# Attention and two MLPs on one core: a planner with shorter bookings for ScalarE and VectorE, and phase three's tanh by halves through one PSUM bank

## The chip, the core and the metric

The kernel runs on one core of a Trainium2 chip. TensorE (PE in the profile) multiplies, VectorE (DVE), ScalarE (ACT) and GpSimd (POOL) work on tiles, and SyncE (SP) issues the transfers; each takes its own instructions strictly in program order. PSUM, where TensorE's products land, is used here as eight banks of 512 fp32 columns. The metric is the device time in microseconds, the median of several executions.

## What is computed

```python
kv = np.einsum('bhsd,bhse->bhde', k, v)            # 8 batches, 8 heads, 576 x 64
out = np.einsum('bhsd,bhde->bhse', q, kv)
rms = np.sqrt(np.mean(out * out, axis=-1, keepdims=True) + 1e-06)
x = (out / rms * g_norm)                           # as 4608 tokens x 512
h = x @ w_in;  x = np.maximum(0.01 * h, h) @ w_out # first MLP, 512 -> 2048 -> 512
h = x @ w_in2; x = (h - np.tanh(h)) @ w_out2       # second MLP
```

## The kernel before

The work stands in four phases, one per weight matrix. Phase one multiplies the normalized attention output by w_in and applies the leaky maximum; phase two multiplies by w_out; phase three multiplies by the second w_in and subtracts the tanh; phase four multiplies by the second w_out. Tokens go in strips of 288 (phases one and two, two strips per batch) or 256 (three and four). Each block product is done with seven products instead of eight, as Strassen does, and each fp32 operand is split into two fp16 parts, a high and a low one, so that a product is three fp16 matmuls per pair of blocks.

The names in the rows: `opa` and `ops` are the split left operands of a strip (ScalarE writes the high part, L576 or L578, VectorE the low one, L583 or L585). `ps_a` to `ps_d` are the PSUM banks that products go to. What a later sum still needs of `ps_a` is copied out by ScalarE (`keep`, L694 to L698: tiles `c`, `u` and `g`); VectorE adds the other banks to those copies (`add`, L707, into `g`). In phase one a bank for `ps_a` comes round again after three products, in phase three too. `wo` is a split of a weight block (ScalarE's high part at L518, `unit` being its input, of which POOL forms differences at L498 to L502).

The attention of batch b is put between phase one's products: `kvd` (L967) is ScalarE's copy of k's product with v, `qt` (L986) its copies of the turned q, `po` (L997) TensorE's product of both, `sq` its square. When a batch is through, the reciprocal roots (`iv`) are written to memory, loaded again spread over the heads (`bc`, L1073), and POOL multiplies the batch's `xg` by them, block by block (L1079, `scale`); then `opa` and `ops` are made from `xg` for that batch's strips.

The order of every engine's program is set at build time by a planner, the class `Plan`. `fit` books a stretch of an engine's calendar for each operation: `dur` is the time that it's given, `over` by how much it may overlap its neighbour, and the operation goes into the first gap that is long enough. `chain` books a list of steps one after the other; each list entry is (engine, duration, function, overlap), "A", "V" and "G" for ScalarE, VectorE and POOL, and None for a pure delay such as a transfer (`LOADBC`, 8 us for `bc`). A function that finds no room in a pool raises NoRoom and is tried again a little later. Instructions are issued in the order of the booked times, so the numbers decide orders and nothing else.

Phase three's strip function is `tanh` (L1423): one ScalarE instruction takes the tanh of four blocks (128x1024) into a tile `th` of the pool L in SBUF, and VectorE subtracts it from `g` in two instructions of 128x512 (L1432). In phase three the banks 0 to 6 hold products; bank 7 is idle there, and phase four uses it.

Of the kernel before, what the change touches and what calls it, by code (L numbers as in the profile page):

```python
# [11 lines left out]
F32 = mybir.dt.float32  # L12
I32 = mybir.dt.int32
AF = mybir.ActivationFunctionType
ALU = mybir.AluOpType
# [14 lines left out]
NOP = 7  # L30
P = 128
# [17 lines left out]
class Plan:  # L49
# [2 lines left out]

    HAND, OVER = 0.25, {"A": 0.6, "V": 0.35, "G": 0.35}

    def __init__(self, delays, dry):
# [9 lines left out]
    def fit(self, eng, t, dur, over=0.0):  # L67


        taken = self.taken[eng]  # L70
        k = max(0, bisect.bisect(taken, (t, 0.0)) - 1)
        while k < len(taken) and taken[k][0] < t + dur - over:
            t = max(t, taken[k][1])
            k += 1
        while k < len(taken) and taken[k][0] < t:
            k += 1
        taken.insert(k, (t, t + dur))
        return t
# [147 lines left out]
def lay_out(plan, nc, pools, sizes, args):  # L226
    q, k, v, g_norm, w1, w2, w3, w4, out = args
    B, H, S, D, NT, DM, DFF = sizes
    NP = DFF // P // 2
# [4 lines left out]
    T2 = 256  # L234
# [8 lines left out]
    L, M, X = (Slots(plan, work, kind, n) for kind, n in (("l", NL), ("m", NM), ("x", NX)))  # L243
    at = plan.at

    used = set()

    def bank(n, name):
        if n in used:
            plan.miss(("bank", n))  # L250
        used.add(n)
        return ps.tile([P, 512], F32, tag=f"p{n}", name=name)

    def free(n):
        used.discard(n)
        plan.met(("bank", n))
# [570 lines left out]
    LOADBC, LOADBC1 = 8.0, 9.0  # L827
# [119 lines left out]
    def pair(b, c, held):  # L947
# [92 lines left out]
        def m_after(e):  # L1040
            if c == PAIRS[-1]:
                norms(b, e)
# [8 lines left out]
    def norms(b, e):  # L1051
        held = {}
# [16 lines left out]
        def load(kk):  # L1069
            held[kk] = L.take([P, 4, T1], F32, "bc", True)  # L1070
            rows = ivd[b].rearrange("(w q) t -> q w t", q=Q)
            for h in range(2):
                nc.sync.dma_start(  # L1073
                    out=held[kk].ap[D * h:D * h + D], in_=rows[2 * kk + h:2 * kk + h + 1].broadcast_to((D, 4, T1))
                )

        def scale(kk, e, n0, n1):
            x = xg[b, kk].ap[:, n0:n1]
            e.tensor_tensor(out=x, in0=x, in1=held[kk].ap[:, n0:n1], op=ALU.mult)  # L1079
            if n1 == 4:  # L1080
                L.give(held[kk])

        x0ops[b] = [{}, {}]
        more = []
        for kk in range(2):
            stages = left_stages(
                lambda kk=kk: xg[b, kk].ap, x0ops[b][kk], None, T1, over=lambda kk=kk: L.give(xg[b, kk]), pieces=2,
                first=None if b else "V", rest=None if b else "V", over_s=() if b else (SOVER,),
            )
            if b == 1:  # L1090
                scaled_ = [("V", 0.66, lambda kk=kk, n=n: scale(kk, nc.vector, n, n + 2)) for n in (0, 2)]
            else:
                scaled_ = [("G", 0.76, lambda kk=kk, n=n: scale(kk, nc.gpsimd, n, n + 1)) for n in range(4 if b else 1)]
            more.append([(None, LOADBC if b > 1 else LOADBC1 if b else 6.0, lambda kk=kk: load(kk))] + scaled_ + stages)

        def wide(kk, n):
            k_ = (4 * kk + n) % 4
# [61 lines left out]
    t = 1.0  # L1159
# [7 lines left out]
    for o in order:  # L1167
        if o[0] == "a":
            held = {}
# [52 lines left out]
    for hp in range(4):  # L1222
        c = PAIRS[hp]
        t_, held = ta[0, c]
# [12 lines left out]
    FIRST = {1: (None,) * EARLY + (0, 8, 16, 24)[:4 - EARLY], 2: (14, 25, 36, 47), 3: (60, 72, 84, 96)}  # L1237
# [3 lines left out]
    for b in range(1, B):  # L1241
        for hp in range(4):
            c = PAIRS[hp]
            n0 = FIRST[b][hp] if b in FIRST else NOP * (NP * b - 16 + 2 * hp) - 2 * (b - 4)
            if n0 is None:
                continue
            held = ta[b, c][1] if (b, c) in ta else {}
            for (dur, fn, after), o in zip(pair(b, c, held), OFFS.get(b, (1, 4, 6, 8, 10, 13))):
                extra.setdefault(n0 + o, []).append((dur, fn, after))
            if b > 1:  # L1250
                loads.append((n0 - 13, b, c, held))
# [168 lines left out]
    spread(lambda i, kk, t: split_late(2, i, kk, t, L, M), UNITS, end1 + 45.0, end2 - 28.0)  # L1420


    def tanh(g, s):  # L1423
        held = {}

        def one():
            held["t"] = L.take([P, 4, T2], F32, "th", True)
            nc.scalar.activation(out=held["t"].ap, in_=g(), func=AF.Tanh)  # L1428

        def two(n):  # L1430
            o = g()[:, 2 * n:2 * n + 2]
            nc.vector.tensor_tensor(out=o, in0=o, in1=held["t"].ap[:, 2 * n:2 * n + 2], op=ALU.subtract)  # L1432

        return [
            ("A", 1.15, one),
            ("V", 0.7, lambda: two(0)), ("V", 0.7, lambda: two(1)),
            (None, 0.0, lambda: L.give(held["t"])),
        ]

    def banks2(n):  # L1440
# [7 lines left out]

    state["rest"] = second_scales(whole, NS2, end2 + 12.0)
    up(1, T2, NS2, x1ops, tanh, lambda s: consts[s][1:3], banks2, ORDER2, between2, freed_to(3, 0.4))  # L1450
    end3 = plan.pe
    c3 = end2 + 0.45 * (end3 - end2)
# [77 lines left out]
```

## Time and profile before

| | |
|---|---|
| time, median of 3 runs | 1490.52 us (1490.04 to 1491.99) |
| profiled execution, its own time | 1495.29 us |
| its span, first to last instruction | 1493.5 us |
| TensorE busy | 1443.8 us (97%), mean granted clock 0.986 |
| VectorE, ScalarE, GpSimd busy | 1245.4 us (83%), 933.7 us (63%), 599.8 us (40%) |

TensorE is busy nearly throughout; 49.7 us of the span are left in which it isn't. The phases lie, by the lines that run in them, at about 0 to 500 us (one, with the attention), 500 to 824 (two), 824 to 1158 (three) and 1158 to the end (four). The profiled execution's own time is 1.8 us above its span and 4.8 us above the median of the unprofiled runs.

### The profile page before, as it was taken

What the parts mean: (1) busy time and instruction counts of PE and PEld (TensorE: products, weight loads), DVE (VectorE), ACT (ScalarE), POOL (GpSimd) and SP (SyncE); (2) the same over time, 40 slices, a digit from 0 to 9 for tenths busy, and PEclk for the clock granted to TensorE, in tenths of its full rate; (3) what the DMA queues carried; (4) which work ended last, traced back from release to release, by engine and by line L of the source; (5) the groups of instructions that cost most, each with busy time, mean ns of one, the idle gap of its engine ahead of it and who ended that gap; (6) DMA issues with size and microseconds to landing.
All of it is one profiled execution on the core that took longest, in us unless ns stands there. A gap on an engine that the chain in (4) does not pass through costs nothing. (4 is left out here: it accounts for less than half of the span.)

```text
span 1493.5 us, 32922 instructions
## 1 busy us (share of the span) xinstructions
PE 1443.8 (97%) x12674; PEld 1195.8 (80%) x12674; DVE 1245.4 (83%) x2029; ACT 933.7 (63%) x1529; POOL 599.8 (40%) x614
## 2 busy tenths in 40 slices
PE   5699999999999999999999999999999999999998
PEld 3467777767777777777777888888888888888887
DVE  4896687677877899999996999989999998888871
ACT  5587777778877644444542677768888555555540
POOL 3141340453643444445542111126577444444430
PEclk8799999999999999999999999999999999999999
DMA  9737898899978745555555856646678744444421
GB/s 281 182 105 228 267 298 263 275 327 306 335 260 300 296 166 191 173 173 200 178 172 198 307 211 221 209 172 221 250 253 320 282 143 154 142 143 146 150 86 36
DMA packets 156461, 321.83 MB, mean 215 GB/s; under 512 B 16656, under 2 KB 98448, under 8 KB 156304
## 3 DMA queue, kind: packets, MB, share of 16 engines
q1 hardware_dynamic: 156304, 319.73, 64.7%
q8 instruction: 99, 1.62, 0.4%
q14 instruction: 58, 0.48, 0.1%
HBM read 189.66 MB, written 130.01 MB: 214 GB/s over the span
## 5 line engine op out<-in xcount | busy, mean ns | idle before, releaser
L639 PEld LDWEIGHTS <-w 128*128 128x128 f16 x8400 | 820.1, 98 | 198.1 <-issue 19.2
L616 POOL TENSOR_TENSOR gl<-gl 128x256 f32<-128x256 f32 (+1 forms) x288 | 322.9, 1122 | 368.3 <-DVE gl L616 132.4
L639 PE MATMUL ps_a<-ops,w 128*128 128x288 f16 (+1 forms) x2400 | 331.7, 282 | 6.5 <-ACT c L696 2.8
L639 PE MATMUL ps_c<-ops,w 128*128 128x288 f16 (+1 forms) x2352 | 314.7, 282 | 2.4 <-DVE g L707 2.3
L639 PE MATMUL ps_a<-opa,w 128*128 128x288 f16 (+1 forms) x2016 | 284.6, 281 | 5.6 <-DVE w L521 4.1
L639 PEld LDWEIGHTS <-ops 128*128 128x128 f16 x1728 | 169.1, 98 | 20.0 <-issue 0.4
L639 PE MATMUL ps_b<-opa,w 128*128 128x288 f16 (+1 forms) x1200 | 175.5, 283 | 0.2 <-DVE r_w L344 0.2
L616 DVE TENSOR_TENSOR gl<-gl 128x288 f32<-128x288 f32 (+1 forms) x256 | 142.4, 558 | 4.3
L616 POOL TENSOR_TENSOR x1g<-x1g 128x256 f32<-128x256 f32 x72 | 69.5, 966 | 172.0 <-PE ps_a L639 109.9
L639 PEld LDWEIGHTS <-opa 128*128 128x128 f16 x1296 | 126.8, 98 | 14.7
L576 ACT ACTIVATE ops<-gl 128x1152 f16<-128x1152 f32 x64 | 74.3, 1161 | 96.2 <-POOL gl L616 96.0
L585 DVE SCALAR_TENSOR_TENSOR ops<-gl,inv,ops 128x1024 f16<-128x1024 f32 x72 | 104.3, 1450 | 28.1 <-ACT ops L578 28.0
L578 ACT ACTIVATE ops<-gl,inv 128x1024 f16<-128x1024 f32 x72 | 82.3, 1144 | 65.7 <-POOL gl L616 65.7
L1432 DVE TENSOR_TENSOR g<-g,th 128x512 f32<-128x512 f32 x144 | 111.9, 787 | 0.9 <-ACT th L1428 0.9
L698 ACT ACTIVATE u<-ps_a,up 128x256 f32<-128x256 f32 x144 | 68.1, 473 | 55.0 <-PE ps_a L639 51.3
L583 DVE TENSOR_TENSOR ops<-gl,ops 128x1152 f16<-128x1152 f32 x64 | 94.2, 1475 | 6.9 <-ACT ops L576 6.9
L707 DVE SCALAR_TENSOR_TENSOR g<-ps_c,u 128x288 f32<-128x288 f32 x128 | 57.9, 452 | 49.2 <-PE ps_c L639 48.5
L639 PE MATMUL ps_c<-w,ops 128*128 128x256 f16 x864 | 97.3, 273 | 0.2 <-DVE osb L707 0.2
L639 PE MATMUL ps_a<-w,ops 128*128 128x256 f16 x864 | 95.8, 273 | 0.0
L1079 POOL TENSOR_TENSOR xg<-xg,bc 128x288 f32<-128x288 f32 x48 | 44.8, 961 | 123.8 <-DMA bc<-iv 55.1
L583 DVE TENSOR_TENSOR opa<-gl,opa 128x864 f16<-128x864 f32 x64 | 81.0, 1266 | 2.0 <-ACT opa L576 1.6
L585 DVE SCALAR_TENSOR_TENSOR opa<-gl,inv,opa 128x768 f16<-128x768 f32 x72 | 79.6, 1106 | 0.8 <-ACT opa L578 0.8
(133 smaller groups left out, 2062.3 us busy)
## 6 DMA issues: line engine op xcount, KB each, us to landing
g<-g SPq DMA_DIRECT2D x64, 576.0 KB, 5.1
gl<-g SPq DMA_DIRECT2D x64, 576.0 KB, 4.5
g<-g SPq DMA_DIRECT2D x72, 512.0 KB, 3.4
gl<-g SPq DMA_DIRECT2D x72, 512.0 KB, 4.2
wd<-wo SPq DMA_DIRECT2D x48, 448.0 KB, 3.4
w<-wd SPq DMA_DIRECT2D x24, 896.0 KB, 8.5
words<-in_moe_w_in_dram SPq DMA_DIRECT2D x64, 256.0 KB, 7.1
words<-in_moe_w_out_dram SPq DMA_DIRECT2D x64, 256.0 KB, 4.5
```

What stands on the lines that cost most here:

```text
L576: nc.scalar.activation(out=o, in_=i_, func=AF.Copy)
L578: nc.scalar.activation(out=o, in_=i_, func=AF.Identity, scale=scale())
L583: nc.vector.tensor_tensor(out=o, in0=i_, in1=h, op=ALU.subtract)
L585: nc.vector.scalar_tensor_tensor(out=o, in0=i_, scalar=scale(), in1=h, op0=ALU.mult, op1=ALU.subtract)
L616: lambda: e.tensor_tensor(out=g()[:, o], in0=g()[:, a], in1=g()[:, b], op=op),
L639: nc.tensor.matmul(out=out_, lhsT=a, rhs=c, start=start and m == 0, stop=stop and m == n - 1, skip_group_check=not fresh,)
L698: nc.scalar.activation(out=t, in_=src, func=AF.Identity, scale=self.scale)
L707: nc.vector.scalar_tensor_tensor(out=o, in0=src, scalar=self.minus if sub else self.scale, in1=t, op0=ALU.mult, op1=ALU.add,)
L1079: e.tensor_tensor(out=x, in0=x, in1=held[kk].ap[:, n0:n1], op=ALU.mult)
L1432: nc.vector.tensor_tensor(out=o, in0=o, in1=held["t"].ap[:, 2 * n:2 * n + 2], op=ALU.subtract)
```

## The change

Four edits, all of numbers and order but the last. (1) In `fit`, for every booking that starts after 130 us of planned time, the stretch and its overlap are multiplied by 0.86 for ScalarE and by 0.92 for VectorE. (2) For the batches 4 to 7 the transfer of `bc` is planned at 9.5 us for 8, and each of POOL's four scalings at 0.95 us for 0.76. (3) The attention of the batches 5, 6 and 7 starts one, two and three products earlier. (4) In phase three the tanh is taken in halves of 128x512; each half goes into PSUM bank 7 and is subtracted from there, and the second half's tanh takes the bank only when the first half's subtraction has given it back. The tile `th` in SBUF is gone. The lines of the changed kernel are four higher from L576 on (eight from the tanh on).

```diff
--- before.py
+++ after.py
@@ -52,6 +52,7 @@
 
 
 
+    SETTLED, PITCH = 130.0, {"A": 0.86, "V": 0.92, "G": 1.0}
     HAND, OVER = 0.25, {"A": 0.6, "V": 0.35, "G": 0.35}
 
     def __init__(self, delays, dry):
@@ -68,6 +69,9 @@
 
 
         taken = self.taken[eng]
+        if t > self.SETTLED:
+            dur *= self.PITCH[eng]
+            over *= self.PITCH[eng]
         k = max(0, bisect.bisect(taken, (t, 0.0)) - 1)
         while k < len(taken) and taken[k][0] < t + dur - over:
             t = max(t, taken[k][1])
@@ -1090,8 +1094,8 @@
             if b == 1:
                 scaled_ = [("V", 0.66, lambda kk=kk, n=n: scale(kk, nc.vector, n, n + 2)) for n in (0, 2)]
             else:
-                scaled_ = [("G", 0.76, lambda kk=kk, n=n: scale(kk, nc.gpsimd, n, n + 1)) for n in range(4 if b else 1)]
-            more.append([(None, LOADBC if b > 1 else LOADBC1 if b else 6.0, lambda kk=kk: load(kk))] + scaled_ + stages)
+                scaled_ = [("G", 0.76 if b < 4 else 0.95, lambda kk=kk, n=n: scale(kk, nc.gpsimd, n, n + 1)) for n in range(4 if b else 1)]
+            more.append([(None, (LOADBC if b < 4 else LOADBC + 1.5) if b > 1 else LOADBC1 if b else 6.0, lambda kk=kk: load(kk))] + scaled_ + stages)
 
         def wide(kk, n):
             k_ = (4 * kk + n) % 4
@@ -1241,7 +1245,7 @@
     for b in range(1, B):
         for hp in range(4):
             c = PAIRS[hp]
-            n0 = FIRST[b][hp] if b in FIRST else NOP * (NP * b - 16 + 2 * hp) - 2 * (b - 4)
+            n0 = FIRST[b][hp] if b in FIRST else NOP * (NP * b - 16 + 2 * hp) - 3 * (b - 4)
             if n0 is None:
                 continue
             held = ta[b, c][1] if (b, c) in ta else {}
@@ -1420,21 +1424,25 @@
     spread(lambda i, kk, t: split_late(2, i, kk, t, L, M), UNITS, end1 + 45.0, end2 - 28.0)
 
 
+    TANH = 7
+
     def tanh(g, s):
         held = {}
 
-        def one():
-            held["t"] = L.take([P, 4, T2], F32, "th", True)
-            nc.scalar.activation(out=held["t"].ap, in_=g(), func=AF.Tanh)
+        def one(n):
+            if TANH in used:
+                raise NoRoom("bank")
+            held[n] = bank(TANH, "th")[:, :2 * T2].rearrange("p (o t) -> p o t", o=2)
+            nc.scalar.activation(out=held[n], in_=g()[:, 2 * n:2 * n + 2], func=AF.Tanh)
 
         def two(n):
             o = g()[:, 2 * n:2 * n + 2]
-            nc.vector.tensor_tensor(out=o, in0=o, in1=held["t"].ap[:, 2 * n:2 * n + 2], op=ALU.subtract)
+            nc.vector.tensor_tensor(out=o, in0=o, in1=held[n], op=ALU.subtract)
+            free(TANH)
 
         return [
-            ("A", 1.15, one),
-            ("V", 0.7, lambda: two(0)), ("V", 0.7, lambda: two(1)),
-            (None, 0.0, lambda: L.give(held["t"])),
+            step for n in range(2)
+            for step in (("A", 0.65, lambda n=n: one(n), 0.5), ("V", 0.65, lambda n=n: two(n), 0.4))
         ]
 
     def banks2(n):
```

What the numbers do to the order is seen on ScalarE in the middle of phase one, where the attention of one batch ends and the operands of its strips are made. In the kernel before:

```order
391 L518 ACTIVATE wo<-unit,s_w_3657 128x896
392 L576 ACTIVATE opa<-xg 128x864
393 L696 ACTIVATE c_4437<-ps_a 128x288
394 L696 ACTIVATE u_4461<-ps_a 128x288
395 L967 ACTIVATE kvd_327<-pk 64x64 x2
396 L1265 ACTIVATE g<-g 128x1152
397 L576 ACTIVATE opa<-xg 128x864
398 L696 ACTIVATE u_4508<-ps_a 128x288
399 L986 ACTIVATE qt<-pq 64x288 x2
400 L696 ACTIVATE g<-ps_a 128x288
401 L518 ACTIVATE wo<-unit,s_w_3657 128x896
402 L986 ACTIVATE qt<-pq 64x288 x2
```

In the changed kernel, at the same place:

```order
390 L522 ACTIVATE wo<-unit,s_w_3653 128x896
391 L700 ACTIVATE g<-ps_a 128x288
392 L971 ACTIVATE kvd_327<-pk 64x64 x2
393 L700 ACTIVATE c_4459<-ps_a 128x288
394 L700 ACTIVATE u_4470<-ps_a 128x288
395 L580 ACTIVATE opa<-xg 128x864
396 L990 ACTIVATE qt<-pq 64x288 x2
397 L1269 ACTIVATE g<-g 128x1152
398 L700 ACTIVATE u_4512<-ps_a 128x288
399 L990 ACTIVATE qt<-pq 64x288 x2
400 L700 ACTIVATE g<-ps_a 128x288
401 L580 ACTIVATE opa<-xg 128x864
```

Both `opa`, which need POOL's scaled `xg`, have moved behind work of the attention and copies out of `ps_a`, and the second `wo` is no longer ahead of the second pair of `qt`. The earlier of such places (the batch before) has changed alike.

At the end of phase one, on ScalarE, before:

```order
612 L576 ACTIVATE opa<-gl 128x864
613 L696 ACTIVATE g<-ps_a 128x288
614 L1265 ACTIVATE g<-g 128x1152
615 L576 ACTIVATE ops<-gl 128x1152
616 L1265 ACTIVATE g<-g 128x1152
```

and in the changed kernel:

```order
612 L580 ACTIVATE ops<-gl 128x1152
613 L700 ACTIVATE u_6785<-ps_a 128x288
614 L580 ACTIVATE opa<-gl 128x864
615 L1269 ACTIVATE g<-g 128x1152
616 L700 ACTIVATE g<-ps_a 128x288
```

The last copy `g` out of `ps_a` stands behind one more instruction, the leaky maximum of 128x1152.

In phase three VectorE's rows (`th` is the tanh, `g<-ps_b` and `g<-ps_c` the sums) before:

```order
1445 L1432 TENSOR_TENSOR g<-g,th 128x512 x2
1446 L707 SCALAR_TENSOR_TENSOR g<-ps_b,up_11120,c_14957 128x256
1447 L585 SCALAR_TENSOR_TENSOR ops<-x1g,s_x_11092,ops 128x512
1448 L1432 TENSOR_TENSOR g<-g,th 128x512
1449 L707 SCALAR_TENSOR_TENSOR g<-ps_c,up_11120,u_15040 128x256
1450 L707 SCALAR_TENSOR_TENSOR g<-ps_c,up_11120,u_14923 128x256
1451 L521 SCALAR_TENSOR_TENSOR wo<-unit,s_w_13307,wo 128x896
```

and in the changed kernel:

```order
1429 L1440 TENSOR_TENSOR g<-g,th 128x512
1430 L711 SCALAR_TENSOR_TENSOR g<-ps_b,up_10543,c_14640 128x256
1431 L1440 TENSOR_TENSOR g<-g,th 128x512
1432 L711 SCALAR_TENSOR_TENSOR g<-ps_c,up_10543,u_14722 128x256
1433 L711 SCALAR_TENSOR_TENSOR g<-ps_c,up_10543,u_14609 128x256
1434 L1440 TENSOR_TENSOR g<-g,th 128x512
1435 L711 SCALAR_TENSOR_TENSOR g<-ps_b,up_10543,c_14710 128x256
```

Between the two subtractions of one strip there stands one sum or more, and on ScalarE the two halves of a strip's tanh have one to three instructions between them.

## Rows read from the trace of the kernel before

**Rows 1.** The page's first part: busy time and share by engine.
```profile
PE 1443.8 (97%) x12674; PEld 1195.8 (80%) x12674; DVE 1245.4 (83%) x2029; ACT 933.7 (63%) x1529; POOL 599.8 (40%) x614
```

**Rows 2.** Busy time by stretch: PE, PEld, DVE, ACT, POOL, clock, DMA share, GB/s.
```profile
95.00:500.00 405.00, 394.58 (x3520) 304.06 (x3518) 305.19 (x557) 314.46 (x603) 161.39 (x180) 0.99 0.90 288
...
824.00:1158.00 334.00, 331.09 (x3024) 295.71 (x3023) 309.95 (x548) 261.50 (x435) 135.66 (x144) 1.00 0.67 240
```

**Rows 3.** What TensorE waited for, 95 to 500 us: total, times, longest.
```profile
PE po L997 <- ACT qt L986: 4.5, 4, 1.9
PE ps_a L639 <- ACT c L696: 2.8, 2, 2.1
...
PE ps_a L639 <- ACT g L696: 0.8, 1, 0.8
```

**Rows 4.** TensorE in order at 276 and at 330 us.
```profile
276.66 0.51 PE L997 MATMUL po<-qt,kvd 128*128 128x288 f32 x1 [1.74 <-ACT qt L986]
...
330.44 1.09 PE L997 MATMUL po<-qt,kvd 128*128 128x288 f32 x2 [1.90 <-ACT qt L986]
```

**Rows 5.** ScalarE in order, 273 to 276 us: start, duration, [idle before, releaser].
```profile
273.55 1.16 ACT L576 ACTIVATE ops<-xg 128x1152 f16<-128x1152 f32 x1 [2.12 <-POOL xg L616]
274.62 0.82 ACT L986 ACTIVATE qt<-pq 64x288 f32<-64x288 f32 x2
```

**Rows 6.** ScalarE in order, 322 to 331 us.
```profile
322.93 0.92 ACT L576 ACTIVATE opa<-xg 128x864 f16<-128x864 f32 x1 [3.41 <-POOL xg L1079]
...
328.92 1.04 ACT L518 ACTIVATE wo<-unit,s_w 128x896 f16<-128x896 f32 x1 [0.56 <-POOL unit L502]
329.98 0.83 ACT L986 ACTIVATE qt<-pq 64x288 f32<-64x288 f32 x2
```

**Rows 7.** The tile `bc`, 300 to 345 us: time from issue to landing.
```profile
DMA to landing us min/median/max: 6.0/7.5/9.0
```

**Rows 8.** Busy time by stretch, behind the wait at 330 us (columns as in rows 2).
```profile
330.80:334.10 3.30, 3.30 (x14) 1.96 (x13) 1.56 (x3) 2.75 (x6) 3.30 (x4) 0.50 1.07 400
```

**Rows 9.** ScalarE in order at 390 us.
```profile
390.47 1.04 ACT L518 ACTIVATE wo<-unit,s_w 128x896 f16<-128x896 f32 x1 [2.98 <-POOL unit L502]
```

**Rows 10.** ScalarE in order, 490 to 492 us.
```profile
490.03 0.93 ACT L576 ACTIVATE opa<-gl 128x864 f16<-128x864 f32 x1 [0.38 <-DMA gl<-g]
490.86 0.39 ACT L696 ACTIVATE g<-ps_a 128x288 f32<-128x288 f32 x1
491.15 1.15 ACT L1265 ACTIVATE g<-g 128x1152 f32<-128x1152 f32 x1
```

**Rows 11.** Groups of instructions by line and shape, 830 to 1160 us: busy, mean ns.
```profile
L1432 DVE TENSOR_TENSOR g<-g,th 128x512 f32<-128x512 f32 x137 | 106.7, 789 | 0.9 <-ACT th L1428 0.9
L707 DVE SCALAR_TENSOR_TENSOR g<-ps_c,up,u 128x256 f32<-128x256 f32 x143 | 65.4, 477 | 13.2 <-PE ps_c L639 9.8
...
L1428 ACT ACTIVATE th<-g 128x1024 f32<-128x1024 f32 x70 | 73.4, 1048 | 1.5 <-DVE g L707 1.4
...
L432 ACT ACTIVATE unit<-words 128x512 f32<-128x512 f32 x12 | 8.0, 670 | 0.0
```

**Rows 12.** Busy time by stretch in phase three (columns as in rows 2).
```profile
950.00:1000.00 50.00, 49.54 (x453) 44.08 (x451) 45.32 (x93) 34.98 (x61) 8.58 (x11) 1.00 0.53 185
...
1100.00:1150.00 50.00, 50.00 (x459) 44.72 (x458) 49.80 (x70) 44.32 (x71) 38.28 (x36) 1.00 0.78 280
```

**Rows 13.** The same stretches, line L1432 alone: VectorE busy (count).
```profile
950.00:1000.00 50.00, 16.49 (x23) 1.00 0.53 185
...
1100.00:1150.00 50.00, 16.37 (x19) 1.00 0.78 280
```

**Rows 14.** One strip's tanh on ScalarE, and its first subtraction on VectorE.
```profile
1146.66 1.04 ACT L1428 ACTIVATE th<-g 128x1024 f32<-128x1024 f32 x1
...
1151.19 0.68 DVE L1432 TENSOR_TENSOR g<-g,th 128x512 f32<-128x512 f32 x1
```

**Rows 15.** What TensorE waited for, 1140 to 1170 us.
```profile
PE ps_c L639 <- DVE g L707: 1.9, 2, 1.5
```

## The prediction, made before the changed kernel ran

> **What bounds the kernel.** I read the busy times first. TensorE works for 1443.8 of 1493.5 us [rows 1], so all that a new order can win is the 49.7 us in which it doesn't, and the time in which it works at half clock. No matmul is added or removed, so neither term of 1443.8 us changes except by the clock. Next, where the idle time lies: from 95 to 500 us it is 405.0 − 394.6 = 10.4 us, and in all of phase three 334.0 − 331.1 = 2.9 us [rows 2]. The first 95 us, before the new bookings begin, are the same in both kernels. So phase one behind 130 us is where the change can pay, and phase three, where three other engines are used most densely, is where it can cost.
>
> Who ends TensorE's waits there: `po` waiting for ScalarE's `qt`, 4.5 us in four waits, the copy `c`, 2.8 us in two, and the copy `g`, 0.8 us in one [rows 3]. The two long ones of `po` are 1.74 us at 274.9 and 1.90 us at 328.5 [rows 4]. ScalarE isn't busy in them for want of speed: it stood still for something else that is ahead in its program. At 273.55 `ops` had waited 2.12 us for POOL's `xg`, and `qt` runs behind it [rows 5]. At 322.93 `opa` had waited 3.41 us for POOL's scaling, and at 328.92 `wo` 0.56 us for POOL's `unit`, again with `qt` next in line [rows 6]. POOL in its turn waits for `bc`, whose transfer takes 6.0 to 9.0 us there, 7.5 in the middle [rows 7], where the plan has 8. So these are waits of a queue's order: work that TensorE needs stands behind work whose data are late.
>
> **The change part by part.** (a) The place at 330 us. Both `opa` are now behind `kvd`, `c`, `u` and the second one also behind both `qt`; the `wo` that waited is no longer ahead of the second `qt`. The first `opa` started 3.41 us after ScalarE was free for it. What moves ahead of it is a `g`, the two `kvd`, a `c` and a `u`, each some 0.4 us as the `qt` at 329.98 is (0.83 us for two, [rows 6]), together some 1.6 us of work in place of idling; and the longer plan for `bc` (9.5) and for the scalings asks for that. Even where `opa` still waits the other 1.8 us, no `c` or `qt` waits with it. I take both TensorE waits as gone: the second is 1.90 us, and the first, which is what is left of 2.8 us for `c` behind the 2.1 us of an earlier place, near 165 us, that the change leaves alone [rows 3], is 0.7 us. Behind the second wait the granted clock was 0.50, that is 1.2 of 2.4 GHz, from 330.8 to 334.1 us with TensorE busy throughout [rows 8]: 3.3 us of work that would take 1.65 at full clock. What TensorE did before the clock fell was to stand still for those 1.90 us. With the wait gone I count the 1.65 us as won. Sum 1.90 + 0.7 + 1.65 = 4.25 us.
>
> (b) The place at 275 us has the same change: `ops` goes behind both pairs of `qt`. 1.74 us won; for the clock I count nothing there.
>
> (c) The place at 390 us: `wo` waited 2.98 us for POOL's `unit` [rows 9], and copies stood behind it. The `wo` stands later in the new order. What `po` lost besides the two long waits is 4.5 − 1.74 − 1.90 = 0.86 us [rows 3, 4]; I count 0.5 of it. Bounds 0 and 0.86.
>
> (d) The end of phase one. The copy `g` ran at 490.86, behind an `opa` that waited for its transfer until 490.03 [rows 10], and TensorE lost 0.8 us to it [rows 3]. Now the leaky maximum, 1.15 us [rows 10], stands between them. If the transfer lands as before, this costs 1.1 us (1.15 less the overlap of neighbours); if `gl` lands earlier since all of the phase is earlier, nothing. I take +1.1, bounds −0.5 and +1.1.
>
> (e) The tanh. ScalarE: 1.048 us for 1024 columns, 0.670 us for 512 by another function [rows 11], so two halves are 1.34 us and each strip costs 0.29 us more, 72 × 0.29 = 21 us in all. ScalarE is busy 35.0 to 44.3 of 50 us there [rows 12], so it has room: 1100 to 1150 us would go to 44.3 + 11 × 0.29 = 47.5. VectorE: the subtraction took 0.789 us in the mean [rows 11], but 16.49/23 = 0.72 us where POOL was busy 8.6 of 50 us, and 16.37/19 = 0.86 us where it was busy 38.3 [rows 12, 13]. An operation that reads PSUM, the sum of 256 columns, took 0.477 us [rows 11]; one of 512 from PSUM isn't in the trace. Bounds: 0.48 (as the sum) and 0.95 (twice the sum); between them I take 0.70, by the row of the same size and nearest kind, the SBUF form with POOL nearly idle (0.72). That gives VectorE 2 × (0.79 − 0.70) = 0.18 us per strip back, 13 us in all.
>
> The Trainium skill, SBUF — State Buffer, section "SBUF: two separate sides", says that a VectorE operation with two SBUF inputs and a GpSimd operation that reads SBUF exclude each other on a shared port; the 0.72 and 0.86 us by POOL's load agree, and by it the subtraction from PSUM should no longer vary with POOL. The Trainium skill, VectorE: DVE Perf Modes, section "The TRN2 errata", speaks against the halves: a fixed cost is paid once per instruction, so that small tiles pay it more often; that agrees with 2 × 0.670 against 1.048 us, and is a loss only if ScalarE or the bank sets the pace.
>
> What the single bank adds is a cycle: half tanh 0.67, subtraction 0.70, half tanh, subtraction, 2.74 us in a strip's 334/72 = 4.64 us. Where VectorE takes up a half late, ScalarE's second half waits, and with it the copies of `ps_a` behind it. VectorE was 49.8 of 50 us busy before the phase's end [rows 12], and there a subtraction began 3.5 us behind its tanh's end (1146.66 + 1.04 to 1151.19, [rows 14]). How much of this lateness is VectorE's chosen order and how much is overdue the trace doesn't say. Bounds for TensorE: nothing, and 9 us (below); I take +0.7, for the last 50 us only.
>
> (f) From phase three to four TensorE waited 1.9 us for sums that VectorE was late with [rows 15]. VectorE is relieved there, so this goes; but the first products of phase four that use bank 7 must wait for the last subtraction from it. I put 1.3 us for that wait (a half tanh and a subtraction, 0.67 + 0.70 = 1.37), between 0.7 (a subtraction alone) and 2. Net −0.6.
>
> **Sum**, in the profiled execution: −4.25 − 1.74 − 0.5 + 1.1 + 0.7 − 0.6 = −5.3 us, from 1495.29 to 1490.0 us. That execution is 4.8 us above the median 1490.52 of the unprofiled ones. Those may have less of these waits to lose, since transfers set them; I take 0.8 us off the gain for it: 1490.5 − 4.5 = **1486.0 us**.
>
> **Rivals.** *The waits only move.* Work that is put behind `qt` comes later itself: `opa` for the next strip, then the first product that reads it. `opa` has the time of several products to spare where the trace shows no wait for it on TensorE, but the transfers stay as late as they were, and the unprofiled runs may not have had the waits at all. Then only half of 4.25 + 1.74 comes, less 1.1 at the end of phase one and 1.7 in phase three: 1490.5 − 3.0 + 2.8 = 1490.3 us, no change. Against it: what is put ahead is work whose data are ready.
>
> *Slower, by bank 7.* If VectorE takes up each half more than (4.64 − 2.74)/2 = 0.95 us late, the strip's cycle is longer than TensorE's strip and VectorE's lateness sets the pace. With 1.15 us late on each half over the 23 strips from 1050 to 1158 us (108/4.64), (2 × 1.15 − 1.90) × 23 = 9.2 us are lost, and with what is won up to the end of phase one (4.25 + 1.74 + 0.5 − 1.1 = 5.4 us) and 1.3 us for the start of phase four it is 1490.5 − 5.4 + 9.2 + 1.3 = 1495.6 us; it decides from 1.1 us late on. For it: the 3.5 us of [rows 14]. Against it: ScalarE's second half stands in its program where VectorE's subtraction is expected, and every strip gives VectorE 0.18 us back.
>
> *More is won.* If VectorE's relief holds in all of phase three, and the place at 164.7 us (2.1 us for `c`, [rows 3], and 1.65 us if the clock falls behind it as in (a)) is dissolved too, the gain is 5.3 + 2.1 + 1.65 + 1.3 = 10.4 us: 1480 us.
>
> **How the numbers follow.** About 0.2% (3 us) is what a measurement of this kernel can tell from no change: faster is below 1487.5, slower above 1493.5 us. I give the forecast 0.5 (own range 1484 to 1489.5 by the bounds of c to f), the moved waits 0.27, bank 7 0.13, the larger gain 0.10. Of the forecast's half 0.43 lies below 1487.5 us and 0.07 in no change; with the 0.10 of the larger gain, faster is 0.53; the moved waits give no change 0.25 more, so 0.32; slower is 0.13 and 0.02 of the moved waits, 0.15. The range 1481 to 1491.5 us leaves out bank 7 and half of the larger gain, under 2 in 10.
>
> **What would show it.** On TensorE from 260 to 340 us no wait of over 1 us for `qt`, and full clock from 330 to 334 us. `opa` and `ops` on ScalarE with next to no idle time before them for POOL. At the end of phase one a wait for the copy `g` of about 2 us, where it was 0.8. In phase three half tanhs of 0.62 to 0.67 us, subtractions near 0.70 us that don't vary with POOL, and TensorE at 50 of 50 us until 1150; waits for `ps_a` on the copies there, with ScalarE idle before the tanh until a subtraction, would say that bank 7 sets the pace. The prediction is wrong if transfers of `bc` simply land later, or if phase three loses more than phase one wins.

## The result and the profile after

The changed kernel took 1512.25 us (median of 4 runs, 1508.49 to 1516.27), 1.0139 times the kernel before (1491.26 us, median of 4 runs; 95% interval of the ratio 1.0109 to 1.0169): about 21 us slower, where 4.5 us faster was forecast and the range ended at 1491.5. The profiled execution took 1512.67 us, its span is 1510.9 us.

To see where, I cut both traces at the same matmuls, those that the kernel before starts at 116.9, 514.8, 823.9, 1158.7 and 1169.6 us: the bulk of phase one, phase two, phase three, the first 11 us of phase four, and its rest to the last matmul. Each number is the difference of two starts, in us.

```
                  phase 1  phase 2  phase 3  start of 4  rest of 4
before             397.93   309.03   334.85       10.92     319.51
after              390.96   317.02   346.33       13.35     319.50
after − before      −6.97    +7.99   +11.48       +2.43      −0.01
```

Ahead of the first of these matmuls the profiled execution was 2.4 us later than before, where the two programs are the same. So phase one gained, in these two executions a little more than the 5.4 us forecast for it, and phases two and three lost 19.5 us, where +0.7 was forecast. How far a phase varies by itself is seen in the traces of the experiments below: without shorter bookings behind 500 us phase two has 309.0 to 309.1 us (but 308.4 in roots_attn), and phase three with the old tanh 334.9 each time; phase one varies more. Nine traces with the changed kernel's program for phase one have 391.0 to 393.1 us, and the two with the program before have 397.9 and 395.5 (tanh_only). So phase one gained between 2.5 and 7 us. Half of the 7.0 is the clock: the kernel before had half clock for 3.4 us at two places, 167 and 331 us, which is worth 3.4 us, and the changed one and tanh_only had it nowhere in the phase.

The page's first part after, to be read beside [rows 1]: TensorE idles 63.3 us instead of 49.7; its busy time, whose ends are modelled, is 3.8 us more.

```profile
PE 1447.6 (96%) x12674; PEld 1195.1 (79%) x12674; DVE 1225.6 (81%) x2029; ACT 931.3 (62%) x1601; POOL 582.5 (39%) x614
```

What TensorE waited for from 95 to 500 us (beside [rows 3]): the long waits for `qt` are gone, and the wait for the copy `g` too.

```profile
PE po L1001 <- ACT qt L990: 1.6, 2, 1.3
PE ps_c L643 <- DVE g L711: 1.5, 1, 1.5
PE ps_a L643 <- ACT c L700: 1.2, 1, 1.2
```

ScalarE in order from 323 us (beside [rows 6]): `opa` runs with no idle time before it, and `qt` right behind. In the stretches below (columns as in rows 2; beside [rows 8]) the granted clock stays full. At 275 us the wait for `qt` is gone too, but behind that place TensorE waits for a sum of VectorE, the last row here.

```profile
323.99 0.92 ACT L580 ACTIVATE opa<-xg 128x864 f16<-128x864 f32 x1
324.81 0.81 ACT L990 ACTIVATE qt<-pq 64x288 f32<-64x288 f32 x2
...
328.30 0.92 ACT L580 ACTIVATE opa<-xg 128x864 f16<-128x864 f32 x1
```
```profile
327.00:330.80 3.80, 3.80 (x29) 2.85 (x28) 2.30 (x5) 3.73 (x10) 3.51 (x5) 1.00 1.05 347
330.80:334.10 3.30, 3.30 (x32) 2.50 (x32) 3.30 (x8) 3.30 (x6) 3.14 (x5) 1.00 1.06 370
```
```profile
282.78 0.90 PE L643 MATMUL ps_c<-ops,w 128*128 128x288 f16 x6 [1.49 <-DVE g L711]
```

Where both kernels have run the same set of matmuls, one can take how far the changed one is ahead since the first cut. By the time of the kernel before that is 1.2 us at 251, 3.1 at 277, 1.0 at 290, 0.8 at 317, 5.4 at 343, 6.5 at 412 and 7.0 at 508 us. So the place at 330 us gave 4.6 us and the one at 390 about 1.1, and what was won at 275 us was lost again within 15 us.

**Phase two.** The waits of TensorE from 500 to 830 us come next, then ScalarE at 648 us, TensorE at the same place, and the stretches of half clock. Before, the waits in the phase were 1.8 us for the copies `u`, the first line here; the `c` of 0.6 us, at the start of phase three, was there too.

```profile
PE ps_a L639 <- ACT u L694: 1.8, 2, 1.2
```
```profile
PE ps_a L643 <- ACT u L698: 3.3, 2, 2.0
PE ps_a L643 <- DVE opa L587: 3.1, 1, 3.1
PE ps_a L643 <- ACT c L702: 0.6, 1, 0.6
PE ps_a L643 <- ACT opa L580: 0.4, 1, 0.4
```
```profile
648.18 1.04 ACT L522 ACTIVATE wo<-unit,s_w 128x896 f16<-128x896 f32 x1 [3.43 <-DVE unit L506]
649.13 1.15 ACT L580 ACTIVATE ops<-gl 128x1152 f16<-128x1152 f32 x1
650.18 0.91 ACT L580 ACTIVATE opa<-gl 128x864 f16<-128x864 f32 x1
...
766.46 1.04 ACT L522 ACTIVATE wo<-unit,s_w 128x896 f16<-128x896 f32 x1 [4.55 <-DVE unit L506]
767.40 1.15 ACT L580 ACTIVATE ops<-gl 128x1152 f16<-128x1152 f32 x1
768.46 0.39 ACT L698 ACTIVATE u<-ps_a 128x288 f32<-128x288 f32 x1
```
```profile
654.52 1.36 PE L643 MATMUL ps_a<-opa,w 128*128 128x288 f16 x5 [3.09 <-DVE opa L587]
```
```profile
654.10:657.40 3.30, 2.88 (x13) 1.77 (x13) 3.30 (x6) 2.98 (x5) 0.00 (x0) 0.50 0.93 335
770.20:773.50 3.30, 3.30 (x15) 2.02 (x14) 3.27 (x5) 1.92 (x3) 0.00 (x0) 0.50 0.88 289
```

A `wo` on ScalarE waits 3.4 and 4.6 us for a difference that VectorE is late with, and the operands and the copy that TensorE needs stand behind it. Such waits alone aren't new: before, `wo` waited 24.3 us for VectorE in the phase, 12 times and up to 4.1 us, and after 21.3 us in 11. New is that at these two places work that TensorE needs at once stands behind them. At the first, VectorE has no idle time either from 644 to 659 us, so how much of the 3.09 us is ScalarE's queue and how much VectorE's own isn't shown. After each of the two long waits (3.09 and 2.03 us) the clock was at half for 3.3 us. Waits of 6.8 us instead of 1.8 and twice about 1.65 us of clock come to 8.3; the phase lost 8.0.

**Phase three.** TensorE's waits from 824 to 1175 us, then ScalarE's for VectorE, after and before. Before, TensorE's only wait for a copy there was the `c` of 0.6 us at the start.

```profile
PE ps_a L643 <- ACT c L702: 9.9, 16, 1.5
```
```profile
ACT th L1436 <- DVE g L1440: 44.1, 47, 3.3
```
```profile
ACT th L1428 <- DVE g L707: 1.4, 4, 0.5
```

One of the sixteen, in order of time on ScalarE, VectorE and TensorE:

```profile
952.24 0.59 ACT L1436 ACTIVATE th<-g 128x512 f32<-128x512 f32 x1
952.76 0.47 ACT L702 ACTIVATE g<-ps_a,up 128x256 f32<-128x256 f32 x1
956.19 0.60 ACT L1436 ACTIVATE th<-g 128x512 f32<-128x512 f32 x1 [2.96 <-DVE g L1440]
956.72 0.46 ACT L702 ACTIVATE c<-ps_a,up 128x256 f32<-128x256 f32 x1
```
```profile
952.82 1.21 DVE L589 SCALAR_TENSOR_TENSOR ops<-x1g,s_x,ops 128x512 f16<-128x512 f32 x1
953.95 1.21 DVE L460 SCALAR_TENSOR_TENSOR unit<-words,unit 128x512 int32<-128x512 int32 x1
955.09 0.47 DVE L711 SCALAR_TENSOR_TENSOR g<-ps_b,up,c 128x256 f32<-128x256 f32 x1
955.48 0.67 DVE L1440 TENSOR_TENSOR g<-g,th 128x512 f32<-128x512 f32 x1
```
```profile
957.23 0.81 PE L643 MATMUL ps_a<-ops,w 128*128 128x256 f16 x6 [1.47 <-ACT c L702]
```

The half tanh that ends at 952.83 is subtracted only from 955.48, behind two operations of 1.21 us and a sum; the other half waits 2.96 us for the bank, the copy `c` stands behind it, and TensorE waits 1.47 us for `c`. The operations themselves were cheaper than forecast (beside [rows 11]):

```profile
L1440 DVE TENSOR_TENSOR g<-g,th 128x512 f32<-128x512 f32 x139 | 94.3, 678 | 7.1 <-ACT th L1436 7.1
L1436 ACT ACTIVATE th<-g 128x512 f32<-128x512 f32 x140 | 83.9, 599 | 44.5 <-DVE g L1440 44.1
```

At the start of phase four TensorE waited 2.3 us for the last subtraction from bank 7:

```profile
PE ps_d L643 <- DVE g L1440: 2.3, 1, 2.3
```

### The profile page after: what moved, and what is told of

Its sections match the earlier page's. It is cut to its first block, busy times and chain, and to the rows that moved or that the text cites. A ratio compares the mean times of both kernels' runs of the same rounds, so it can differ in the third digit from the quotient of the medians.

```text
span 1510.9 us, 32816 instructions
## 1 busy us (share of the span) xinstructions
PE 1447.6 (96%) x12674; PEld 1195.1 (79%) x12674; DVE 1225.6 (81%) x2029; ACT 931.3 (62%) x1601; POOL 582.5 (39%) x614
## 4 chain that ended last, share of the span: by engine, by line
PE 41%; DVE 11%; issue 4%; ACT 3%; POOL 1%; DMA 1%; DVEq 0%; SPq 0%; ACTq 0%; POOLq 0%
PE ps_a L643 19%; PE ps_c L643 11%; PE ps_b L643 6%; PE ps_d L643 4%; DVE opa L587 2%; DVE g L1440 2%; DVE g L711 2%; DVE ops L589 1%; DVE gl L620 1%; POOL gl L620 1%; ACT ops L580 1%; DVE wo L525 1%; DVE opa L589 1%; DVE ops L587 1%; ACT th L1436 0%
## 5 line engine op out<-in xcount | busy, mean ns | idle before, releaser
L620 POOL TENSOR_TENSOR x1g<-x1g 128x256 f32<-128x256 f32 x72 | 62.3, 866 | 187.9 <-DVE opa L589 171.6
L1436 ACT ACTIVATE th<-g 128x512 f32<-128x512 f32 x144 | 86.3, 599 | 48.7 <-DVE g L1440 48.3
L1440 DVE TENSOR_TENSOR g<-g,th 128x512 f32<-128x512 f32 x144 | 97.7, 678 | 8.1 <-ACT th L1436 8.1
L589 DVE SCALAR_TENSOR_TENSOR ops<-gl,inv,ops 128x1024 f16<-128x1024 f32 x72 | 96.5, 1341 | 8.7 <-ACT ops L582 8.6
L711 DVE SCALAR_TENSOR_TENSOR g<-ps_c,up,u 128x256 f32<-128x256 f32 x144 | 67.1, 479 | 25.6 <-PE ps_c L643 20.2
```

Of the source, the lines that this page charges most:

```text
L589: nc.vector.scalar_tensor_tensor(out=o, in0=i_, scalar=scale(), in1=h, op0=ALU.mult, op1=ALU.subtract)
L620: lambda: e.tensor_tensor(out=g()[:, o], in0=g()[:, a], in1=g()[:, b], op=op),
L711: nc.vector.scalar_tensor_tensor(out=o, in0=src, scalar=self.minus if sub else self.scale, in1=t, op0=ALU.mult, op1=ALU.add,)
L1436: nc.scalar.activation(out=held[n], in_=g()[:, 2 * n:2 * n + 2], func=AF.Tanh)
L1440: nc.vector.tensor_tensor(out=o, in0=o, in1=held[n], op=ALU.subtract)
```

## The experiments

Each ran beside the kernel before on the same chip. In the table the ratio is to that, with its interval, and the phases are cut as above, from one profiled execution each. In the rows a line of the program has a number up to eight higher or lower from kernel to kernel.

```
                 median   ratio (95%)              ph 1    ph 2    ph 3   start 4
tanh_only       1502.74  1.0056 (1.0037-1.0075)  395.51  309.08  342.95   12.59
no_tanh         1501.37  1.0051 (1.0034-1.0068)  391.56  315.19  339.48   10.92
p1_no_tanh      1487.22  0.9960 (0.9940-0.9979)  392.08  309.03  334.87   10.92
p1_tanh         1499.75  1.0039 (1.0026-1.0051)  391.76  309.09  342.86   12.59
p1_tanh_sbuf    1491.82  0.9989 (0.9970-1.0007)  392.19  309.05  336.63   10.92
p1_tanh_late    1500.93  1.0046 (1.0031-1.0061)  393.05  309.04  344.38   12.59
p1_tanh_mix     1489.24  0.9967 (0.9952-0.9982)  392.30  309.04  332.82   12.41
late_A          1494.74  1.0004 (0.9984-1.0024)  392.88  309.80  339.32   10.92
late_V          1494.00  0.9997 (0.9980-1.0015)  392.19  311.35  335.83   10.92
p1_pitch        1496.05  1.0014 (0.9996-1.0033)  399.33  309.04  334.87   10.92
roots_only      1486.21  0.9948 (0.9931-0.9964)  392.55  309.05  334.88   10.92
attn_only       1503.64  1.0053 (1.0033-1.0073)  406.24  309.05  334.88   10.92
roots_attn      1502.71  1.0052 (1.0031-1.0073)  403.24  308.38  334.87   10.92
p1_pitch_roots  1490.96  0.9979 (0.9963-0.9994)  392.76  309.02  334.86   10.92
p1_pitch_attn   1495.72  1.0006 (0.9988-1.0024)  397.44  309.02  334.87   10.92
roots_mix       1486.03  0.9944 (0.9925-0.9963)  389.64  309.00  332.81   10.92
```

**The change taken apart.** tanh_only is the kernel before with edit 4 alone; no_tanh the changed kernel without it; the other two end the shorter bookings with phase one:

```diff
-        if t > self.SETTLED:
+        if self.SETTLED < t < 500.0:
```

> The kernel before with the tanh by halves through bank 7 alone; bookings, roots and attention as before. Theory A (the single bank itself makes phase three slow, since the copies of ps_a stand behind a half tanh that waits for VectorE): +10 to +14 us over the kernel before, some 40 waits of the half tanh for the subtraction. Rival B (the bank costs only because VectorE's shorter bookings make it late): within 3 us of the kernel before.

> The changed kernel with the old tanh in SBUF: shorter bookings, roots and attention changed. Theory A: phase three costs as before, so what is left is phase one won (about -5) and phase two lost (about +7): 0 to +4 us over the kernel before. Rival B (the shorter bookings cost in phase three whatever the tanh is): +6 or more.

> As no_tanh, but the shorter bookings end at 500 us of planned time, so that phases two to four are planned as before. If the loss of phase two comes from the shorter bookings: -4 to -7 us against the kernel before, no wait of 3 us at 650 us. If phase two loses for another reason (what phase one leaves behind): 0 to +4 us.

> The changed kernel, tanh by halves included, with the shorter bookings ending at 500 us of planned time. Theory A (the bank): 10 to 14 us more than p1_no_tanh. Rival B (bank and shorter bookings together): at most 3 us more than p1_no_tanh.

The tanh costs phase three 8.1 us by itself (342.95), with no shorter booking anywhere. In the whole that is 8 us (1.0056 of the kernel before), under theory A's 10 to 14 and far over rival B's 3: the bank doesn't need the shorter bookings to cost. Between p1_tanh and p1_no_tanh it is 12.5 us by the medians, 9.7 by the phases. In no_tanh it was the rival's forecast that came true (+6 or more): shorter bookings behind phase one cost 6.2 us in phase two and 4.6 in phase three by themselves, and nothing is left of it where they end at 500 us (309.03 and 334.87). The tanh and the shorter bookings together cost phase three 11.5, nearly the sum of 12.7. The rest of phase four was 2.5 us longer in no_tanh too, as in late_V and, at 3.0, in p1_tanh_sbuf, but not in the changed kernel; its cause is open. Of the 8.0 us that phase two lost in the changed kernel, 1.8 more than in no_tanh, 1.7 is the clock: no_tanh has the same two long waits (3.10 and 2.03 us), but half clock, for 3.4 us, behind the first alone. In tanh_only the waits of phase three, the last one at the start of four:

```profile
PE ps_a L639 <- ACT c L698: 4.3, 10, 0.8
PE ps_a L639 <- ACT u L698: 3.1, 6, 1.2
PE ps_d L639 <- DVE g L1436: 1.5, 1, 1.5
```

**The bank or the halves.** p1_tanh_sbuf keeps the four steps, with one tile in SBUF for both halves; p1_tanh_late puts 1.2 us of planned time between the halves; p1_tanh_mix uses the bank for the first half alone.

```diff
 p1_tanh_sbuf
-            if TANH in used:
-                raise NoRoom("bank")
-            held[n] = bank(TANH, "th")[:, :2 * T2].rearrange("p (o t) -> p o t", o=2)
+            if n == 0:
+                held["t"] = L.take([P, 4, T2], F32, "th", True)
+            held[n] = held["t"].ap[:, 2 * n:2 * n + 2]
 ... (and the tile is given back behind the second subtraction)
 p1_tanh_late
 ...
+        return halves[0] + [(None, 1.2, lambda: None)] + halves[1]
 p1_tanh_mix
 ... (the first half as in the changed kernel)
+            else:
+                held["t"] = L.take([P, 4, T2], F32, "th", True)
+                held[n] = held["t"].ap[:, :2]
 ...
```

> As p1_tanh (shorter bookings to 500 us, tanh by halves), but both halves in one tile in SBUF as before, so that the second half's tanh does not wait for the first half's subtraction. Theory A (the shared bank is what phase three pays): phase three back near 335 us, no wait of the half tanh for VectorE, the whole within 3 us of p1_no_tanh. Rival B (the halves pay: 21 us more on ScalarE and the planner's order with four steps): phase three stays at 340 to 343 us.

> As p1_tanh (tanh by halves through bank 7), with 1.2 us of planned time more between the first half's subtraction and the second half's tanh, so that fewer copies of ps_a stand behind a half tanh that waits for a late VectorE. Theory A (what phase three pays is the copies behind the waiting half): phase three 336 to 340 us, against 342.9. Rival B (the cycle through one bank is too long for a strip, wherever its halves stand): 343 us or more.

> As p1_tanh, but the first half's tanh goes to bank 7 and the second half's to a tile in SBUF, so that the bank is used once per strip. Theory A (the wait of a half tanh for the other half's subtraction is what phase three pays): 335 to 338 us for phase three, under 10 us of waits of the tanh for VectorE. Rival B (any use of bank 7 for the tanh costs it): 340 us or more.

Without the wait for the bank phase three is at 336.6 us: the halves cost 1.8 in this form, the bank's sharing 6.2. (The rest of phase four was 3.0 us longer in that kernel, so the whole stays 4.6 us above p1_no_tanh and not within 3.) Used once per strip the same bank costs nothing there, and phase three is 2.0 us shorter than before (332.8); the start of phase four still pays 1.5. The later second half didn't help (344.4): theory A's remedy failed there, and rival B's 343 or more came true. But B's reason, a cycle too long for a strip, isn't what the operations take (2 × (0.600 + 0.680) = 2.56 of 4.64 us); the waits for VectorE make it long. ScalarE's waits for VectorE in phase three, p1_tanh_late first, then p1_tanh_mix:

```profile
ACT th L1436 <- DVE g L1440: 48.2, 71, 2.0
```
```profile
ACT th L1440 <- DVE g L1444: 5.9, 10, 1.3
```

So where the second half stands in the plan changes which copies stand behind a wait, not that nearly every strip has one. The subtraction in p1_tanh_sbuf, both operands in SBUF, and in p1_tanh_mix, where every second one has an operand in PSUM:

```profile
L1440 DVE TENSOR_TENSOR g<-g,th 128x512 f32<-128x512 f32 x144 | 115.1, 805 | 0.5 <-ACT th L1436 0.5
```
```profile
L1444 DVE TENSOR_TENSOR g<-g,th 128x512 f32<-128x512 f32 x142 | 101.9, 723 | 0.5 <-ACT th L1440 0.5
```

**Which engine's bookings.** late_A and late_V are no_tanh with only one engine's bookings shorter behind 500 us ("V" for "A" in late_V).

```diff
-        if t > self.SETTLED:
+        if t > self.SETTLED and (t < 500.0 or eng == "A"):
```

> As no_tanh, but behind 500 us only ScalarE's bookings are shorter. Theory C (the loss of phases two and three comes from VectorE, which is booked for less than it needs where it is busy nearly all the time): near p1_no_tanh, within 3 us. Rival D (ScalarE's shorter bookings put waits for POOL and VectorE ahead of copies): 5 us or more above p1_no_tanh.

> As no_tanh, but behind 500 us only VectorE's bookings are shorter. Theory C: near no_tanh, 10 to 14 us above p1_no_tanh. Rival D: within 3 us of p1_no_tanh.

Neither theory holds. Phase two lost 0.8 us by ScalarE's bookings, 2.3 by VectorE's and 6.2 by both, of which 1.7 is the clock; the wait of 3.1 us at 650 us comes only with both. Phase three lost 4.5 by ScalarE's, 1.0 by VectorE's and 4.6 by both. Each is about 7 us slower than p1_no_tanh, in medians of runs beside different sets of the kernel before. Why the two phases differ in this is open.

**What gained in phase one.** The three other edits, alone and in pairs, with the old tanh and no shorter bookings behind 500 us: p1_pitch has edit 1 alone, roots_only edit 2, attn_only edit 3.

```diff
 roots_only
-                scaled_ = [("G", 0.76, lambda ...
+                scaled_ = [("G", 0.76 if b < 4 else 0.95, lambda ...
-            more.append([(None, LOADBC if b > 1 ...
+            more.append([(None, (LOADBC if b < 4 else LOADBC + 1.5) if b > 1 ...
 attn_only
-... NOP * (NP * b - 16 + 2 * hp) - 2 * (b - 4)
+... NOP * (NP * b - 16 + 2 * hp) - 3 * (b - 4)
```

> The kernel before with the shorter bookings up to 500 us alone; roots, attention and tanh as before. If the shorter bookings made the gain of phase one: phase one 391 to 393 us as in p1_no_tanh, -5 to -7 us in all. If the roots' bookings and the earlier attention made it: phase one near 397 us, within 2 us of the kernel before.

> The kernel before with the roots' longer bookings and the earlier attention alone; no shorter bookings anywhere, the old tanh. Theory E (these two made the gain of phase one, since the shorter bookings alone made none): phase one 391 to 393 us, the whole 4 to 7 us below the kernel before. Rival F (it takes the shorter bookings together with them): phase one 395 us or more.

> The kernel before with the roots' longer bookings alone. If opa and ops stand later in ScalarE's program by these bookings: waits for qt at 270 to 340 us gone, phase one 392 to 394 us. If the earlier attention does it: phase one 397 us or more.

> The kernel before with the attention of batches 5 to 7 one to three products earlier, alone. If the earlier attention gives the roots' transfers their time: phase one 392 to 394 us. If the roots' bookings do it: 397 us or more.

> The kernel before with shorter bookings to 500 us and the roots' longer bookings; attention and tanh as before. If the roots' bookings carry the gain: phase one 391 to 394 us. If the gain needs the earlier attention beside the shorter bookings: 396 us or more.

> The kernel before with shorter bookings to 500 us and the earlier attention; the roots and the tanh as before. If the roots' bookings carry the gain: phase one 398 us or more. If the shorter bookings undo what the earlier attention costs and more: 391 to 394 us.

Phase one took 397.93 us before, 399.3 with the shorter bookings, 392.6 with the roots' bookings and 406.2 with the earlier attention. With the roots' bookings in, phase one is at 392 to 393 us unless the earlier attention comes without the shorter bookings (403.2); all three give 392.1 (p1_no_tanh). In the whole, roots_only is 0.9948 of the kernel before and p1_no_tanh 0.9960, but p1_pitch_roots only 0.9979. So the roots' bookings carry the gain, the earlier attention costs 8 us, and the shorter bookings take that back. Whether p1_pitch loses anything in the whole can't be told (1.0014, from 0.9996). Waits from 100 to 500 us in roots_only, then in attn_only:

```profile
PE pk L957 <- DMA v<-in_v_dram: 2.8, 1, 2.8
PE ps_a L640 <- ACT c L697: 2.1, 1, 2.1
...
PE po L998 <- ACT qt L987: 0.7, 2, 0.4
```
```profile
PE po L998 <- ACT qt L987: 3.7, 5, 2.3
PE ps_c L640 <- DVE g L708: 3.5, 6, 1.0
PE ps_a L640 <- ACT c L697: 2.9, 2, 1.8
PE ps_a L640 <- ACT ops L577: 1.7, 1, 1.7
```

In roots_only the waits for `qt` fell from 4.5 to 0.7 us; the wait for `c` near 165 us is the one that was there before. Its longest wait, 2.8 us at 379 us for the transfer of `v`, is new, and half clock for 3.4 us stood behind it: counted at the same matmuls roots_only was 8.3 us ahead of the kernel before at 386 us and 5.3 at 398. That wait also stands in roots_mix (1.5 us), p1_tanh_mix (1.1) and p1_pitch_roots (0.7). In attn_only the waits for `qt` stay, and TensorE waits for operands (`ops`) as well. They stay in p1_pitch_roots too (4.7 us, at other places), so that kernel's phase one isn't explained by them.

**What gained, together.** roots_mix is roots_only with the tanh of p1_tanh_mix, but for the last eight tiles, which keep the whole tanh in SBUF.

> The kernel before with the roots' longer bookings, and the tanh by halves, the first in bank 7 and the second in SBUF, but for the last eight tiles, which take the whole tanh in SBUF as before; no shorter bookings, attention as before. If the gains add up: phase one 392 to 394, phase three 333 to 334, the start of phase four 10.9 us; 6 to 9 us below the kernel before in its phases. If the bank must be kept for phase four longer than that: 12.4 us at the start of phase four.

The gains add up by phases, and the start of phase four is as before: 0.9944 of the kernel before. Phase one, at 389.6 us, is under the forecast, with the program of roots_only (392.6): the wait for `v` was 1.3 us shorter and no half clock stood behind it. roots_only, with two numbers changed, is at 0.9948; the two can't be told apart by these runs.

## Why the prediction was wrong

The first step that failed was to leave phase two out: the text said that the change can pay in phase one and can cost in phase three, and gave the shorter bookings no term anywhere else. They cost 8.0 us in phase two here, 6.2 without the new tanh, and 4.6 in phase three without it. By the trace the cost in phase two is again a queue's order: at 648 and 766 us ScalarE's program reaches a `wo` before VectorE has made its input, with work for TensorE behind it, and this is what part (a) had described for POOL. That the shorter bookings make it is shown by the runs that end them at 500 us; which of the shorter numbers puts that work there isn't.

The second was the size of the single bank in (e). The step "Bounds for TensorE: nothing, and 9 us; I take +0.7, for the last 50 us only" took a value near the lower bound; it measured +8.1 alone and +11.5 with the shorter bookings. The mechanism is that of the rival by bank 7, which had 0.13: VectorE takes a half up late, ScalarE waits, and copies of `ps_a` stand behind it. But the rival's condition was wrong. It asked that each half be over 0.95 us late, so that the strip's cycle outgrew TensorE's strip, from 1050 us on. The cycle was shorter than thought (2 × (0.599 + 0.678) = 2.55 us of 4.64), both halves were that late in only 6 of the 72 strips (5 in p1_tanh), and the loss came all the same, from 829 us on in p1_tanh and from 846 after: here one late half, there another, with a copy behind it out of a bank that TensorE needs three products later. The 3.5 us in [rows 14] was no exception of the phase's end: in the 41 strips of the kernel before where the trace leaves no doubt which subtraction is a tanh's first, VectorE began it 1.3 us behind the tanh's end in the mean, and in 19 of them over 0.95 us. The tile in SBUF had hidden that.

The forecast's own range left (e) out as well. By the text's own bounds of (c) to (f) the 1486.0 us go from 1482.7 to 1495.5 us, and not from 1484 to 1489.5; the 9 us of (e) stood in the rival alone.

Part by part:
- (a): right in size. No wait for `qt` over 1.3 us remains, the half clock at 330 us is gone, and 4.6 us were won there, where 1.90 + 1.65 and 0.7 were forecast. The 1.65 us are in part luck: in tanh_only, with the program before, the clock stayed full behind the same wait. Its cause was in edit 2, which the text named ("the longer plan for `bc`"), and roots_only shows it; the shorter bookings and the earlier attention, alone, gained nothing.
- (b): the wait for `qt` went, but not its price. The changed kernel waited 1.49 us at 281 us for VectorE's sum and kept nothing of the 1.74 (p1_no_tanh and p1_tanh kept 0.5 and 0.8). This is the rival of the waits that only move, at one place. In roots_only 2.3 us were won there and kept.
- (c): about 1.1 us, where 0.5 was taken and 0.86 was the bound.
- (d): wrong. The wait for the copy `g` at the phase's end didn't grow, it went; TensorE lost 0.4 us there, for a transfer. With the same program for phase one that wait is 0.4 to 1.3 us in four other traces (1.3 in p1_tanh), never the 2 us that the text expected.
- (e), the operations: a half tanh 0.599 us where 0.670 was taken, a subtraction 0.678 where 0.70 was. It varied from 669 to 691 ns over phase three, while the SBUF form in p1_tanh_sbuf had a mean of 805. The Trainium skill, SBUF — State Buffer, section "SBUF: two separate sides", says that a VectorE operation with two SBUF inputs and a GpSimd operation that reads SBUF shut each other out of a shared port. The trace fits this: with one operand in PSUM the subtraction varied by 22 ns. On ScalarE two half tanhs took 2 × 0.599 − 1.048 = 0.15 us per strip more than the whole one, and 0.20 in p1_tanh_sbuf, where they too went to SBUF (0.623 each); 0.29 was taken. The Trainium skill, VectorE: DVE Perf Modes, section "The TRN2 errata", says that operations with a source in SBUF pay a fixed cost once per instruction, and the trace agrees with that. Whether it is part of the 1.8 us that the halves cost phase three in p1_tanh_sbuf no run shows.
- (f): TensorE waited 2.3 us for bank 7 (1.5 in tanh_only), where 1.3 was taken, with 2 as the upper bound; the 1.9 us for VectorE's sums did go.

What stays open: why the earlier attention costs 8 us alone and nothing with the shorter bookings, why those bookings and the roots' together gain less (0.9979) than the roots' alone, and how the two engines' bookings share the loss of phases two and three. That the copies behind a waiting half tanh are what TensorE pays is read from the trace; the runs show that the loss goes when the second half doesn't need the bank.

## What to carry to other kernels

A buffer that two engines hand back and forth makes the one wait for the other's lateness; before taking a tile from a pool down to one place, read in the trace how late the consumer takes it up, in every strip and not in one, and count every wait with what stands behind it in the producer's queue, not only whether the cycle fits. Shorter bookings in a planner are an edit of every phase: each phase needs its own term. When a late input blocks a queue, correct the plan's number for that input (here `bc` and the scalings); alone it made this kernel 0.5% faster, where the whole change made it 1.4% slower. A gain that hangs on the clock behind one wait is read from more than one execution.

## What the runs showed that was not expected

The tanh of 512 columns took 0.599 us into PSUM and 0.623 us into SBUF (p1_tanh_sbuf), less than the 0.670 us of another function of the same size on ScalarE [rows 11]. And the granted clock fell to 0.50 behind TensorE's waits of 3.09 and 2.03 us in phase two, while it stayed full behind 1.49 us at 281.3 and behind the many waits of 0.3 to 1.5 us in phase three. But the same wait didn't always have the same sequel: in no_tanh the clock stayed full behind the 2.03 us, and in tanh_only, whose program in phase one is that of the kernel before, it stayed full behind 2.06 and 2.48 us, where it had fallen behind 2.13 and 1.90. In p1_pitch it stayed full behind 3.23 us. So in these traces the length of the wait alone doesn't say whether the clock falls. TensorE's wait in tanh_only, and the stretch behind it, to be read beside [rows 4] and [rows 8]:

```profile
329.55 0.75 PE L997 MATMUL po<-qt,kvd 128*128 128x288 f32 x2 [2.48 <-ACT qt L986]
```
```profile
329.50:333.00 3.50, 3.45 (x24) 2.62 (x25) 3.02 (x7) 3.34 (x7) 3.42 (x5) 1.00 1.07 407
```
